# Rest-row scores in four wide matmuls in place of sixteen narrow ones, and no spare products at the turn of the first memory half

## The chip, the cores and the metric

The kernel runs on one NeuronCore of one Trainium2 chip. The metric is device time in microseconds, lower is better; the time before is 2300.26 us, the median of three runs (2291.55 to 2302.47). Every operand in HBM and the output are bf16; sums are in fp32.

## The reference

The output mixes two branches, row by row, with a gate g = sigmoid of x times a vector. Branch B is a feed-forward layer: (gelu(x Wg) * (x Wu)) Wd, 1024 to 3584 and back, over 2048 rows. Branch A is the one that the change touches. It is a recurrence over 64 segments of 32 rows with a memory of 8 rows, 32 heads of 128:

```python
mem = mem0
for s in range(n_seg):                       # 64 segments
    xs = x[:, s*32:(s+1)*32, :]
    h = concatenate([mem, xs], axis=1)       # 8 + 32 = 40 rows
    q, k, v = h @ Wq, h @ Wk, h @ Wv         # 32 heads of 128
    scores = (q . k) * 128**-0.5             # 40 x 40 for each head
    scores = where(mask, scores, -1e9)       # causal; the memory rows see all
    o = (softmax(scores) @ v) @ Wo
    mem = o[:, :8, :]                        # feeds the next segment
    outs.append(o[:, 8:, :])
return g * concatenate(outs) + (1 - g) * B
```

A segment needs the memory rows of the one before, so the segments run one after the other, and for each one all of Wq, Wk, Wv and Wo (8 MB each) passes through the core, as far as it isn't resident.

## The kernel before

The program is written as a list of operations in an order laid out by hand; a small tracker adds semaphore waits from the regions that each operation reads and writes, and each engine then runs its own operations in that order.

**Rows.** Of a segment's 40 rows, 32 go through the recurrent projections: 24 rows of x (`NR`) and the 8 memory rows, in `hT`. The other 8 rows of x, the "rest" (`NB`), need no memory for q, k and v; they are projected for four segments at a time by `fill` (lines 835 to 845; the matmuls stand on L841) from `hR`, leave through `fill_evac` and `fill_put`, lie in HBM scratch (`qk_scr`, `v_scr`) and come back for a segment as `qkr` and `vB`. In `qkr` and `kT` the last columns belong to these rest rows.

**Halves and order.** The 32 heads are two halves of 16. A head in a half has two indices, j and g (0 to 3 each): g is the group of 32 PE columns and 32 PSUM partitions in which it is computed, j its place along the free axis. A segment walks through the stages k, q, (second part of o of the segment before), v for the first half, then k, q, o, v, o for the other. `walk` lists these steps, `proj` (L771 for k, q and v, L787 and L804 for o) issues the matmuls of a step, and `plan(s)` hangs everything else on a step with `on(...)`. Weights stream in 512 KB pieces on the SP queue as their slots come free; 8 matmuls deep, four column groups run side by side with 32 rows of h as the stationary operand.

**Scores.** `scores(u)` works on one half: 16 heads in the PSUM bank `SS`, 128 partitions by four blocks (one for each j) of 80 columns. In block j, columns 0 to 39 are the 32 recurrent rows of head (j, g) against its 40 keys, on partitions 32g to 32g+31; columns 40 to 79 are its 8 rest rows, on partitions 32g to 32g+7. `mask` (L687) first writes the mask `mS` into all four blocks by a matmul with the identity, then 16 matmuls of 32 rows and 16 of 8 rows, 40 columns each, add the products (L700). The softmax is two reductions, an add, an exponential and two products over 128x320 (L706 to L714). DVE then transposes the probabilities in blocks of 32x32, in two instructions of 128x256 (L720): `pAB` has the columns of the recurrent keys in its first half and those of the rest keys in its second, and in `tAB` the queries of head (j, g) must stand at columns 64j to 64j+39 of each half, where `attend` takes them as the moving operand (L729 with `vA`, L737 with `vB`). `attend` for a segment's first half of heads is hung on the first step of o, the scores on the last step of v ahead of it; between them PE runs 68 matmuls of the projections. For the second half they are hung on ("o", 0, 4) and ("o", 1, 0).

**The turn.** When o of a segment is done, `fold(s, b)` adds the two partial sums of one memory half on DVE (L815, L816) and `next_mem(s, b)` transposes it on PE (L825) and copies it into the next `hT` (L828), which the next segment's k needs. At the turn of the first memory half, ahead of step ("k", 0, 0) of the next segment, `plan` puts more work between these: where a segment has two fills, the eight fill matmul groups of the second in two portions of four; in the other 33 of the 63 turns the spare products, `warm(5)` and `warm(2)` (L847 to L855, matmuls on L851): 20 and 8 matmuls of 128x32 by 128x512 whose result in bank `B0` nobody reads.

After the recurrence the rest rows go through Wo (L1027), and then branch B runs in four blocks of 512 rows (L1077, L1131, L1112), with the gate's mix at its ends.

Of the kernel before, what the change touches and what calls it, by code (L numbers as in the profile page):

```python
# [8 lines left out]
ALU = mybir.AluOpType  # L9
# [201 lines left out]
def bass_gated_mix__memory_aug_recurrent_mem_tr__geglu_ffn__prompt_kernel(  # L211
# [21 lines left out]
    NB = SEG - NR  # L233
# [7 lines left out]
    NEG = -1.0e9  # L241
    LQ = 40
# [3 lines left out]
    with ExitStack() as es:  # L246
# [20 lines left out]
        PB = [es.enter_context(nc.psum_tensor(f"pb{i}", [128, 512], FP32)) for i in range(8)]  # L267
# [197 lines left out]
        for g in range(4):  # L465
            q = slice(32 * g, 32 * g + 32)


            pw(mS, lambda e, q=q: sel(e, mS[q, 0:NR], ALU.is_ge, NEG, 0, [[-1, NR]], 1))
            pw(mS, lambda e, q=q: sel(e, mS[q, 32:40], ALU.is_ge, NEG, -NR, [[0, NB]], 1))  # L470

            pw(mS, lambda e, q=q: sel(e, mS[q, 72:80], ALU.is_ge, NEG, 0, [[-1, NB]], 1))
        op("act", lambda e: e.preload_act_table_set("natural_log_exp_and_others"))


# [10 lines left out]
        assert cur[0] <= top  # L486
        memT = al("memT", [128, 64], at=oRc.off)

        def tr_mem(e):
            for kc in range(KC):  # L490
                ins = e.transpose(PBV[5][:, kc * 8:(kc + 1) * 8], pm[0:8, kc * 128:(kc + 1) * 128], ident[0:8, 0:8])
            return ins
# [58 lines left out]
        for n in range(8):  # L551
            first(at_step(0, "k", 0, n))
            if n + 3 < NPX:
                load_x(n + 3)
        op("pe", tr_mem, rd=[pm.r(), ident.r()], wr=[BK(5)])
        op("dve", lambda e: e.tensor_copy(memT[:, :], PBV[5][:, 0:64]), rd=[BK(5)], wr=[memT.r()])
        do_x(0)
        load_h(0, "pool")
# [132 lines left out]
        def scores(u, masked=True):  # L691
            if not masked:
                mask()

            def f(e):
                for n, c in ((32, 0), (8, 40)):
                    for j in range(4):
                        for g in range(4):
                            x = 8 * (4 * j + g)
                            ins = e.matmul(PB[SS][32 * g:32 * g + n, j * 80 + c:j * 80 + c + LQ],  # L700
                                           lhsT=qT[:, j, g, :] if n == 32 else qkr[:, 2 * u, x:x + 8],
                                           rhs=kT[:, j, g, :], start=False, stop=True, skip_group_check=True)
                return ins
            op("pe", f, rd=[qT.r(), qkr.r(256 * u, 256 * u + 128), kT.r()], wr=[BK(SS)])
            op("pool", lambda e: e.memset(pAB[:, 256:544].bitcast(FP32), 0.0), wr=[pAB.r(256)])
            op("dve", lambda e: e.tensor_reduce(nm, sS, AX.X, ALU.max, negate=True), rd=[BK(SS)], wr=[st8.r(0, 8)])  # L706
            op("dve", lambda e: e.tensor_tensor(out=sS, in0=sS, in1=b8(nm, LQ), op=ALU.add), rd=[BK(SS), st8.r(0, 8)], wr=[BK(SS)])  # L707
            op("act", lambda e: e.activation(E8[:, :, :].rearrange("p a c -> p (a c)"), PB[SS][:, 0:320], ACTF.Exp, scale=scale),  # L708
               rd=[BK(SS)], wr=[E8.r()])
            op("dve", lambda e: e.tensor_reduce(sm, E8[:, :, :], AX.X, ALU.add), rd=[E8.r()], wr=[st8.r(8, 16)])  # L710
            op("dve", lambda e: e.reciprocal(sm, sm), rd=[st8.r(8, 16)], wr=[st8.r(8, 16)])
            op("dve", lambda e: e.tensor_tensor(out=pAB[:, 0:256].rearrange("p (a c) -> p a c", a=8), in0=E8[:, :, 0:32], in1=b8(sm, 32), op=ALU.mult),
               rd=[E8.r(), st8.r(8, 16)], wr=[pAB.r(0, 256)])
            fin = op("dve", lambda e: e.tensor_tensor(  # L714
                out=pAB[:, 256:544].rearrange("p (j a) -> p j a", j=4)[:, :, 0:64].rearrange("p j (c k) -> p j c k", c=2)[:, :, :, 0:8],
                in0=E8[:, :, 32:40].rearrange("p (j c) k -> p j c k", c=2),
                in1=sm.rearrange("p (j c) -> p j c", c=2).unsqueeze(3).to_broadcast([128, 4, 2, 8]), op=ALU.mult),
               rd=[E8.r(), st8.r(8, 16)], wr=[pAB.r(256)])
            for c in (0, 256):
                op("dve", lambda e, c=c: e.transpose(tAB[:, c:c + 256], pAB[:, c:c + 256]), rd=[pAB.r(c, c + 256)], wr=[tAB.r(c, c + 256)], after=[fin])  # L720

        def attend(u, by=((2, "act"), (3, "dve"), (0, "act"), (1, "dve")), b3=SS):
            bo = (B0, B1, B2, b3)
# [120 lines left out]
                out.append(lambda f=f, w=w: op("pe", f, rd=[h.r(), w.r()], wr=[BK(b)]))  # L844
            return out

        def warm(n):  # L847
            def f(e):
                for x in range(4 * n):
                    g = x % 4  # L850
                    ins = e.matmul(PB[B0][32 * g:32 * g + 32, :], lhsT=hR[:, 7, :], rhs=spare[:, g * 512:(g + 1) * 512],  # L851
                                   start=True, stop=True)
                return ins
            spare = slots[home["q", 0, 7]]
            op("pe", f, rd=[hR.r(224), spare.r()], wr=[BK(B0)])  # L855

        def fill_evac(m, u, G, b, st):
            st = stage[st]
            if m == "v":
                act_copy(st[:, :], PB[b][:, :], [BK(b)], [st.r()])  # L860
                for g in range(4):
                    op("pool", lambda e, g=g: e.dma_start(
                        v_scr[4 * G:4 * G + 4, :, 4 * g:4 * g + 4, u, :].rearrange("s i j c -> (s i) j c"),
                        st[32 * g:32 * g + 32, :].rearrange("p (j c) -> p j c", j=4)), rd=[st.r()], wr=[("D", "v", G, g, u)], lane=f"fv{g}")
            else:
                act_copy(st[:, :], PB[b][:, :], [BK(b)], [st.r()])

        def fill_put(m, u, G, st, bank=TT):
            if m == "v":
                return  # L870
            st = stage[st]
            turn(st, bank)
            op("dve", lambda e: e.tensor_copy(st[:, :].rearrange("p (i x c) -> p x i c", i=4, x=16),
                                              PBV[bank][:, 0:512].rearrange("p (x i c) -> p x i c", x=16, i=4)), rd=[BK(bank)], wr=[st.r()])
            m4 = 3 * u if m == "q" else 1 + u
            op("pool", lambda e: e.dma_start(qk_scr[:, 4 * G:4 * G + 4, m4, :], st[:, :].rearrange("p (i y) -> p i y", i=4)),
               rd=[st.r()], wr=[("D", "qk", G, m, u)], lane="fq")
# [14 lines left out]
        def some(fs, n):  # L892
            return lambda: run(fs, n)
# [6 lines left out]
        def plan(s):  # L900
# [8 lines left out]
            def on(m, r, n, *fs, s=s):  # L909
                at.setdefault((s, m, r, n), []).extend(fs)  # L910
# [80 lines left out]
                return  # L991
            nx = dict(s=s + 1)
            on("k", 0, 0, lambda: fold(s, 0), **nx)
            on("k", 0, 0, some(f2, 4) if two else lambda: warm(5), **nx)
            on("k", 0, 0, lambda: next_mem(s, 0), **nx)
            on("k", 0, 0, some(f2, 4) if two else lambda: warm(2), **nx)
            if two:
                on("k", 0, 0, lambda: fill_evac(*fl[1], B0, ua), **nx)
            on("q", 0, 2, lambda: fold(s, 1), **nx)
            if two:  # L1000
# [175 lines left out]
```

## Time and profile before

| what | value |
|---|---|
| median of three runs | 2300.26 us |
| the profiled execution, as timed | 2308.1 us |
| its span, first to last instruction | 2306.3 us |
| mean granted PE clock | 0.983 |
| HBM read and written | 596.85 MB and 36.63 MB |
| 200 to 1650 us: PE busy, DMA share, rate | 1345.9 of 1450 us, 0.93, 334 GB/s |
| L700, rest rows: 2048 matmuls | 37.4 us busy |
| L700, recurrent rows: 2048 matmuls | 37.1 us busy |
| L851, spare products: 924 matmuls | 64.6 us busy |
| L720, DVE transposes: 256 | 98.7 us busy, 424 ns each |

A busy time is the time in which at least one instruction of the group ran; matmuls overlap, four column groups at a time, so 4096 matmuls of some 180 ns each make far less than their sum. "Idle before" in a group's row is the engine's own idle time ahead of it, with what released it; a name with "issue" means that nothing in the profile held the engine up.

The span has three parts: the start, to some 120 us; the recurrence, to some 1650 us, about 24 us for a segment; and branch B with the rest rows' projection, where PE runs long matmuls back to back.

### The profile page before, as it was taken

What the parts mean: (1) busy time and instruction counts of PE and PEld (TensorE: products, weight loads), DVE (VectorE), ACT (ScalarE), POOL (GpSimd) and SP (SyncE); (2) the same over time, 40 slices, a digit from 0 to 9 for tenths busy, and PEclk for the clock granted to TensorE, in tenths of its full rate; (3) what the DMA queues carried; (4) which work ended last, traced back from release to release, by engine and by line L of the source; (5) the groups of instructions that cost most, each with busy time, mean ns of one, the idle gap of its engine ahead of it and who ended that gap; (6) DMA issues with size and microseconds to landing.
All of it is one profiled execution on the core that took longest, in us unless ns stands there. A gap on an engine that the chain in (4) does not pass through costs nothing.

```text
span 2306.3 us, 74586 instructions
## 1 busy us (share of the span) xinstructions
PE 2119.9 (92%) x33852; PEld 1048.7 (45%) x33852; DVE 1028.8 (45%) x2440; ACT 541.4 (23%) x1111; POOL 423.7 (18%) x821
## 2 busy tenths in 40 slices
PE   4598999999999999999999999998899999999999
PEld 2244444444444444444444444444464444444444
DVE  3343444454444444544444444454316446163462
ACT  1122222222222222222222222221113123032130
POOL 4422212222222222222222222221100000000000
PEclk8799999999999999999999999999899999999999
DMA  9989999898998999999989899999964440903520
GB/s 375 354 298 327 334 341 358 321 354 320 327 330 325 340 336 316 344 325 355 332 325 354 312 331 341 317 340 324 342 204 143 150 151 10 291 20 125 172 87 19
DMA packets 237579, 638.34 MB, mean 277 GB/s; under 512 B 22440, under 2 KB 91304, under 8 KB 230480
## 3 DMA queue, kind: packets, MB, share of 16 engines
q1 hardware_dynamic: 213440, 596.58, 72.4%
q0 software_dynamic: 13888, 26.31, 3.5%
q10 hardware_dynamic: 9936, 10.69, 1.4%
q8 instruction: 266, 4.36, 0.8%
q14 instruction: 49, 0.40, 0.0%
HBM read 596.85 MB, written 36.63 MB: 275 GB/s over the span
## 4 chain that ended last, share of the span: by engine, by line
PE 70%; DMA 19%; issue 4%; DVE 4%; ACT 2%; POOL 1%; ACTq 0%; SPq 0%; POOLq 0%
PE pb L771 23%; PE pb L1077 15%; DMA sl<-in_A_Wv_dram 7%; PE pb L1131 5%; PE pb L841 5%; PE pb L804 4%; PE pb L787 4%; PE pb L673 3%; DMA qkr<-qk_scr 3%; PE pb L1027 3%; PE pb L1112 2%; PE pb L851 2%; DMA wall<-wg_scr 2%; DMA xr_scr<-xr 1%; DMA o_scr<-oRc 1%
## 5 line engine op out<-in xcount | busy, mean ns | idle before, releaser
L771 PE MATMUL pb<-sl,hT 128*32 128x512 bf16 x12288 | 778.4, 383 | 28.8 <-issue 16.9
L771 PEld LDWEIGHTS pb<-sl,hT 128*32 128x32 bf16 x12288 | 337.5, 97 | 331.6 <-issue 50.8
L841 PE MATMUL pb<-sl,hR 128*32 128x512 bf16 x3072 | 225.3, 392 | 4.1 <-issue 3.2
L1077 PE MATMUL pb<-xT,wg 128*128 128x512 bf16 x896 | 211.7, 379 | 0.7
L1077 PE MATMUL pb<-xT,wu 128*128 128x512 bf16 x896 | 211.7, 379 | 0.0
L804 PE MATMUL pb<-wall,oT 128*32 128x256 bf16 x4056 | 150.9, 275 | 22.9 <-issue 8.5
L787 PE MATMUL pb<-wall,oT 128*32 128x512 bf16 x2048 | 152.4, 387 | 17.1 <-issue 9.5
L656 ACT ACTIVATE kS<-pb 128x512 bf16<-128x512 f32 x127 | 75.8, 597 | 384.3 <-PE pb L771 364.9
L815 DVE COPY part<-pb 64x256 f32<-64x256 f32 x128 | 54.0, 422 | 247.9 <-PE pb L804 246.9
L754 POOL COPY oRc<-oT 128x128 bf16<-128x128 bf16 x128 | 96.4, 753 | 359.2 <-DVE oT L659 357.0
L1131 PE MATMUL pb<-wd,GT 128*128 128x512 bf16 x672 | 146.0, 379 | 1.7 <-DMA wd<-in_B_w_down_dram 1.7
L1085 ACT ACTIVATE s<-pb 128x512 f32<-128x512 f32 x112 | 66.8, 596 | 311.9 <-PE pb L1077 311.9
L708 ACT ACTIVATE E<-pb 128x320 bf16<-128x320 f32 x128 | 55.9, 437 | 352.9 <-DVE pb L707 352.9
L1077 PEld LDWEIGHTS pb<-xT,wg 128*128 128x128 bf16 x896 | 87.2, 98 | 108.0 <-DVE GT L1093 3.7
L1077 PEld LDWEIGHTS pb<-xT,wu 128*128 128x128 bf16 x896 | 87.7, 98 | 105.7
L804 PEld LDWEIGHTS pb<-wall,oT 128*32 128x32 bf16 x4056 | 100.6, 96 | 74.9 <-ACT oT L656 25.9
L1086 DVE SCALAR_TENSOR_TENSOR tp<-s,pb 128x512 f32<-128x512 f32 x112 | 77.0, 687 | 124.2 <-ACT s L1085 124.0
L659 DVE CAST oT<-pb 128x160 bf16<-128x160 f32 x256 | 76.5, 320 | 111.7 <-PE pb L737 111.7
L659 DVE COPY kT<-pb 128x512 bf16<-128x512 bf16 x128 | 54.4, 425 | 159.8 <-PE pb L673 159.5
L880 POOL COPY kT<-qkr 128x128 bf16<-128x128 bf16 x128 | 37.3, 291 | 466.3 <-DVE kT L659 222.6
L841 PEld LDWEIGHTS pb<-sl,hR 128*32 128x32 bf16 x3072 | 82.3, 98 | 70.7 <-issue 20.8
L1090 DVE SCALAR_TENSOR_TENSOR tp<-tp,pb 128x512 f32<-128x512 f32 x112 | 77.1, 688 | 78.6 <-ACT tp L1089 78.6
(100 smaller groups left out, 2286.8 us busy)
## 6 DMA issues: line engine op xcount, KB each, us to landing
sl<-in_A_Wv_dram SPq DMA_DIRECT2D x128, 1024.0 KB, 10.8
wall<-wg_scr SPq DMA_DIRECT2D x53, 1536.0 KB, 9.2
sl<-in_A_Wk_dram SPq DMA_DIRECT2D x64, 1024.0 KB, 5.9
sl<-in_A_Wq_dram SPq DMA_DIRECT2D x64, 1024.0 KB, 9.0
wall<-wo_scr SPq DMA_DIRECT2D x120, 512.0 KB, 6.0
wd<-in_B_w_down_dram SPq DMA_DIRECT2D x42, 1024.0 KB, 5.4
sl<-in_A_Wv_dram SPq DMA_DIRECT2D x75, 512.0 KB, 11.1
wall<-in_A_Wo_dram SPq DMA_DIRECT2D x41, 512.0 KB, 7.9
```

The costliest lines, as they stand in the source:

```text
L656: op("act", lambda e: e.activation(o, i, ACTF.Copy), rd=rd, wr=wr)
L659: op("dve", lambda e: e.tensor_copy(o, i), rd=rd, wr=wr, after=after)
L673: ins = e.transpose(PBV[bank][:, j * 128:(j + 1) * 128], st[:, j * 128:(j + 1) * 128], ident[:, :])
L754: op("pool", lambda e: e.tensor_copy(oRc[:, :, 16 * u:16 * u + 16].rearrange("p c x -> p x c"), oT[:, :, :, 32:40].rearrange("p g j c -> p ...
L771: ins = e.matmul(PB[bk][32 * g:32 * g + 32, :], lhsT=h[:, i, :], rhs=w[:, g * 512:(g + 1) * 512], start=(n == 0), stop=(n == 7))
L787: ins = e.matmul(PB[XO][32 * g:32 * g + 32, :], lhsT=oT[:, j, x, 0:32], rhs=wall[:, na:nb + 1:nb - na, c:c + 256], start=(n == 0 and hp == 0),
L804: ins = e.matmul(PB[XO][32 * g:32 * g + 32, 256 * b:256 * b + 256], lhsT=oT[:, j, x, 0:32], rhs=w[:, c:c + 256], start=False, stop=(n % 4 ...
L841: ins = e.matmul(PB[b][32 * g:32 * g + 32, :], lhsT=h[:, k[2], :], rhs=w[:, g * 512:(g + 1) * 512], start=(n == 0), stop=(n == 7))
L1077: ins = e.matmul(PB[bk][:, 0:FB], lhsT=w[:, kc, cc:cc + 128], rhs=xT[:, :, :, kc, :].rearrange("p t i c -> p (t i) c"), start=(kc == 0), s ...
L1086: op("dve", lambda e, hg=hg, t=t: e.scalar_tensor_tensor(out=t[:, :], in0=s1[:, :], scalar=1.0, in1=hg, op0=ALU.add, op1=ALU.mult), rd=[BK ...
L1090: op("dve", lambda e, hu=hu, t=t: e.scalar_tensor_tensor(out=t[:, :], in0=t[:, :], scalar=1.0, in1=hu, op0=ALU.add, op1=ALU.mult), rd=[BK( ...
L1131: ins = e.matmul(PB[bank[2 * k + hf]][:, :], lhsT=GT[:, j, tb * 128:(tb + 1) * 128], rhs=w[:, jj, hf * 512:(hf + 1) * 512], start=(j == 0) ...
```

## The change

Three things.

1. The rest rows of a half are no longer scored head by head. For each column group g one matmul has all 32 rest rows of its four heads (8 rows each, j = 0 to 3) as the stationary operand and the 160 keys of the four heads as the moving one, and writes columns 40 to 79 of all four blocks. Of its 32 rows in block j only rows 8j to 8j+7 are head j's own; the others are products across heads that nobody uses. Sixteen matmuls with their weight loads become four. So that the rows stand like that, `fill_put` copies q in the order (segment, g, j, row) in place of (segment, j, g, row); k keeps its order.
2. With the rest rows at partitions 32g+8j in block j, the mask has to hold for all 16 groups of 8 partitions (`mT`, made once on POOL, transposed on PE with `tr_mem` and copied to `mS`; four POOL selections go), and the transposes have to shift them: `halves` transposes the rest part of each half first, with a target stride of 56 columns, so that the rows of head j land at 64j+32, and then the recurrent part at 64j, over what was written too much. Two DVE instructions of 128x256 become four of 128x128. The second of a pair waits for the first.
3. `warm` is gone: in the 33 turns without a second fill nothing stands between `fold`, `next_mem` and the next k.

```diff
@@ -469,7 +469,6 @@
             pw(mS, lambda e, q=q: sel(e, mS[q, 0:NR], ALU.is_ge, NEG, 0, [[-1, NR]], 1))
             pw(mS, lambda e, q=q: sel(e, mS[q, 32:40], ALU.is_ge, NEG, -NR, [[0, NB]], 1))
 
-            pw(mS, lambda e, q=q: sel(e, mS[q, 72:80], ALU.is_ge, NEG, 0, [[-1, NB]], 1))
         op("act", lambda e: e.preload_act_table_set("natural_log_exp_and_others"))
 
 
@@ -486,7 +485,12 @@
         assert cur[0] <= top
         memT = al("memT", [128, 64], at=oRc.off)
 
+        mT = al("mT", [128, 16, NB])
+        pw(mT, lambda e: e.memset(mT[0:NB, :, :], 0.0), True)
+        pw(mT, lambda e: sel(e, mT[0:NB, :, :], ALU.is_ge, NEG, 0, [[0, 16], [1, NB]], -1))
+
         def tr_mem(e):
+            e.transpose(PBV[5][:, 64:64 + NB], mT[0:NB, :, :].rearrange("p x i -> p (x i)"), ident[0:NB, 0:NB])
             for kc in range(KC):
                 ins = e.transpose(PBV[5][:, kc * 8:(kc + 1) * 8], pm[0:8, kc * 128:(kc + 1) * 128], ident[0:8, 0:8])
             return ins
@@ -552,7 +556,8 @@
             first(at_step(0, "k", 0, n))
             if n + 3 < NPX:
                 load_x(n + 3)
-        op("pe", tr_mem, rd=[pm.r(), ident.r()], wr=[BK(5)])
+        op("pe", tr_mem, rd=[pm.r(), mT.r(), ident.r()], wr=[BK(5)])
+        op("dve", lambda e: e.tensor_copy(mS[:, 72:80], PBV[5][:, 64:64 + NB]), rd=[BK(5)], wr=[mS.r(72, 80)])
         op("dve", lambda e: e.tensor_copy(memT[:, :], PBV[5][:, 0:64]), rd=[BK(5)], wr=[memT.r()])
         do_x(0)
         load_h(0, "pool")
@@ -693,13 +698,14 @@
                 mask()
 
             def f(e):
-                for n, c in ((32, 0), (8, 40)):
-                    for j in range(4):
-                        for g in range(4):
-                            x = 8 * (4 * j + g)
-                            ins = e.matmul(PB[SS][32 * g:32 * g + n, j * 80 + c:j * 80 + c + LQ],
-                                           lhsT=qT[:, j, g, :] if n == 32 else qkr[:, 2 * u, x:x + 8],
-                                           rhs=kT[:, j, g, :], start=False, stop=True, skip_group_check=True)
+                for j in range(4):
+                    for g in range(4):
+                        ins = e.matmul(PB[SS][32 * g:32 * g + 32, j * 80:j * 80 + LQ], lhsT=qT[:, j, g, :],
+                                       rhs=kT[:, j, g, :], start=False, stop=True, skip_group_check=True)
+                for g in range(4):
+                    ins = e.matmul(PB[SS][32 * g:32 * g + 32, 0:320].rearrange("p (j c) -> p j c", j=4)[:, :, LQ:80],
+                                   lhsT=qkr[:, 2 * u, 32 * g:32 * g + 32],
+                                   rhs=kT[:, :, g, :], start=False, stop=True, skip_group_check=True)
                 return ins
             op("pe", f, rd=[qT.r(), qkr.r(256 * u, 256 * u + 128), kT.r()], wr=[BK(SS)])
             op("pool", lambda e: e.memset(pAB[:, 256:544].bitcast(FP32), 0.0), wr=[pAB.r(256)])
@@ -716,8 +722,11 @@
                 in0=E8[:, :, 32:40].rearrange("p (j c) k -> p j c k", c=2),
                 in1=sm.rearrange("p (j c) -> p j c", c=2).unsqueeze(3).to_broadcast([128, 4, 2, 8]), op=ALU.mult),
                rd=[E8.r(), st8.r(8, 16)], wr=[pAB.r(256)])
-            for c in (0, 256):
-                op("dve", lambda e, c=c: e.transpose(tAB[:, c:c + 256], pAB[:, c:c + 256]), rd=[pAB.r(c, c + 256)], wr=[tAB.r(c, c + 256)], after=[fin])
+            def halves(k, w, after):
+                return [op("dve", lambda e, c=c: e.transpose(tAB[:, c + 32 * k:c + 32 * k + 4 * w].rearrange("p (j x) -> p j x", j=4)[:, :, 0:32],
+                                                             pAB[:, c:c + 256].rearrange("p (j k x) -> p j k x", j=4, k=2)[:, :, k, :]),
+                           rd=[pAB.r(c, c + 256)], wr=[tAB.r(c, c + 256)], after=[x]) for c, x in zip((0, 256), after)]
+            halves(0, 64, halves(1, 56, [fin, fin]))
 
         def attend(u, by=((2, "act"), (3, "dve"), (0, "act"), (1, "dve")), b3=SS):
             bo = (B0, B1, B2, b3)
@@ -844,16 +853,6 @@
                 out.append(lambda f=f, w=w: op("pe", f, rd=[h.r(), w.r()], wr=[BK(b)]))
             return out
 
-        def warm(n):
-            def f(e):
-                for x in range(4 * n):
-                    g = x % 4
-                    ins = e.matmul(PB[B0][32 * g:32 * g + 32, :], lhsT=hR[:, 7, :], rhs=spare[:, g * 512:(g + 1) * 512],
-                                   start=True, stop=True)
-                return ins
-            spare = slots[home["q", 0, 7]]
-            op("pe", f, rd=[hR.r(224), spare.r()], wr=[BK(B0)])
-
         def fill_evac(m, u, G, b, st):
             st = stage[st]
             if m == "v":
@@ -870,8 +869,8 @@
                 return
             st = stage[st]
             turn(st, bank)
-            op("dve", lambda e: e.tensor_copy(st[:, :].rearrange("p (i x c) -> p x i c", i=4, x=16),
-                                              PBV[bank][:, 0:512].rearrange("p (x i c) -> p x i c", x=16, i=4)), rd=[BK(bank)], wr=[st.r()])
+            to = st[:, :].rearrange("p (i g j c) -> p j g i c", i=4, g=4, j=4) if m == "q" else st[:, :].rearrange("p (i j g c) -> p j g i c", i=4, j=4, g=4)
+            op("dve", lambda e: e.tensor_copy(to, PBV[bank][:, 0:512].rearrange("p (j g i c) -> p j g i c", j=4, g=4, i=4)), rd=[BK(bank)], wr=[st.r()])
             m4 = 3 * u if m == "q" else 1 + u
             op("pool", lambda e: e.dma_start(qk_scr[:, 4 * G:4 * G + 4, m4, :], st[:, :].rearrange("p (i y) -> p i y", i=4)),
                rd=[st.r()], wr=[("D", "qk", G, m, u)], lane="fq")
@@ -991,10 +990,11 @@
                 return
             nx = dict(s=s + 1)
             on("k", 0, 0, lambda: fold(s, 0), **nx)
-            on("k", 0, 0, some(f2, 4) if two else lambda: warm(5), **nx)
+            if two:
+                on("k", 0, 0, some(f2, 4), **nx)
             on("k", 0, 0, lambda: next_mem(s, 0), **nx)
-            on("k", 0, 0, some(f2, 4) if two else lambda: warm(2), **nx)
             if two:
+                on("k", 0, 0, some(f2, 4), **nx)
                 on("k", 0, 0, lambda: fill_evac(*fl[1], B0, ua), **nx)
             on("q", 0, 2, lambda: fold(s, 1), **nx)
             if two:
```

## The prediction

> **What bounds the kernel now.** I read the page first, then PE's waits, then the timeline of single stretches. The page:
>
> ```profile
> PE 2119.9 (92%) x33852; PEld 1048.7 (45%) x33852; DVE 1028.8 (45%) x2440; ACT 541.4 (23%) x1111; POOL 423.7 (18%) x821
> ...
> DMA  9989999898998999999989899999964440903520
> ...
> q8 instruction: 266, 4.36, 0.8%
> ```
>
> PE is busy for 92% of the span of 2306.3 us, and in the recurrence (to about 1650 us) the DMA engines are nearly full beside it. The line that matters most is the smallest: 266 instruction packets. 4.36 MB over 266 is 16 KB each; 33852 matmuls and 33852 weight loads are 67704 instructions, and 67704 over 266 is about 255. PE's program comes in blocks of some 256 instructions, one packet for each. What that costs is in PE's waits, among rows for other causes:
>
> ```profile
> PE pb L771 <- issue: 16.9, 20, 1.9
> ...
> PE pb L787 <- issue: 9.5, 8, 2.4
> PE pb L804 <- issue: 9.0, 12, 1.7
> PE pb L700 <- issue: 8.7, 10, 2.2
> ```
>
> "Issue" means that nothing in the profile held PE up. With L841 (3.2, 5 times), L673 (3.1, 4) and L737 (2.9, 3) these are 53.3 us in 62 waits, more than any engine or DMA costs PE. That they are block boundaries shows on the timeline of PE:
>
> ```profile
> 762.24 1.91 PE L771 MATMUL pb<-sl,hT 128*32 128x512 bf16 x31 [1.69 <-issue]
> ...
> 768.57 0.61 PE L851 MATMUL pb<-sl,hR 128*32 128x512 bf16 x6 [0.34 <-issue]
> ```
>
> Between these two waits PE runs 127 matmuls with their loads, one block to within a few. They strike whatever line stands there, so their price depends on how long a block lasts, not on what PE computes. Do they reach the end? From the end of one turn to the next (starts of L816) a segment without such a wait takes 22.72 us (791.32 to 814.04); the one with the wait of 2.40 takes 26.78 (837.26 to 864.04), of which 1.66 is the half clock seen below. So they pass through almost whole; over segments 11 to 60 I find 0.94 us of period for 1 us of wait.
>
> **Fewer instructions (both edits).** The spare products go in 33 turns: 28 matmuls and 28 loads each, 1848. In each of 128 score steps 16 pairs for the rest rows become 4: 24 instructions less, 3072. Together 4920 of 67704, 19 packets. Nearly all lie in the recurrence, where 226 packets cover 1460 us (190 to 1650), 6.46 us a block, 6.2 without the waits. About 18 blocks fewer there stretch a block to some 6.75, by 0.5. If a packet takes as long to come as now, each of the 62 waits is shorter by 0.5, 31 us at most; about 18 of them are shorter than that and give only their length, which leaves 28. A packet queues behind the weight loads, and the loads get denser as PE gets faster, so I take **-24**. Bounds: 0 (packets later by as much) and -45 (all but the longest waits).
> The Trainium skill, Runtime: NRT & Kernel Launch, "Instruction fetch mechanics", gives the same 16 KB blocks of 256 instructions and says that crossing one is mostly hidden; the rows above disagree, with 53.3 us unhidden. By the page this term would be 0.
>
> **The turn of the first half.** PE waits for fold and next_mem; the spare products fill the wait:
>
> ```profile
> 790.52 1.25 PE L851 MATMUL pb<-sl,hR 128*32 128x512 bf16 x20
> 791.32 0.42 DVE L816 TENSOR_TENSOR a_bf<-pb,part 64x256 bf16<-64x256 f32 x1
> 791.79 0.23 PE L825 MATMUL pb<-ident,a_bf 64*128 64x64 bf16 x2
> 791.95 0.61 PE L851 MATMUL pb<-sl,hR 128*32 128x512 bf16 x8
> 792.06 0.18 DVE L828 COPY hT<-pb 128x32 bf16<-128x32 bf16 x1 [0.32 <-PE pb L825]
> 792.39 0.60 PE L771 MATMUL pb<-sl,hT 128*32 128x512 bf16 x8
> ```
>
> The first twenty cost nothing: L825 starts 0.05 after L816 ends, at best 0.03 is to be had. The eight behind it cost 0.10: L771 starts 0.15 after L828 ends, a wait alone takes 0.05. 33 turns x 0.10, and 0.03 in about 20 of them: **-4** (bounds -7, where a half clock lengthened the products themselves at 181 and 1608 us, and 0).
> What they hid is PE's clock. A stretch of 3.4 us with little matmul work is followed by one at half clock:
>
> ```profile
> 540.24:543.65 3.41, 1.46 (x31) 0.57 (x23) 2.31 (x7) 0.44 (x1) 0.09 (x1) 1.00 1.05 398
> 854.28:857.68 3.40, 1.00 (x21) 0.60 (x23) 2.27 (x7) 0.44 (x1) 0.05 (x1) 1.00 1.04 395
> 857.69:861.09 3.40, 3.40 (x40) 1.58 (x32) 0.00 (x0) 0.04 (x1) 0.00 (x0) 0.50 1.02 426
> ```
>
> Columns: length, busy PE, PEld, DVE, ACT, POOL, clock, DMA share, GB/s. PE idle for 2.40 of 3.40 halves the next stretch; 1.95 idle did not. There are three such half stretches from 190 to 1650 us (687, 858, 1605), each behind an issue wait. A turn without the products idles 1.35 (790.69 to 791.76, 792.02 to 792.30), so it needs 0.6 to 1 more in the same stretch. Laying the shorter waits at random over the segments I expect five half stretches in place of three: 2 x 1.5 us, **+3**. Bounds: -4 (none left) and +48 (each of the 33 turns, 1.45 each).
> The Trainium skill, TensorE: Matmul & The Clock Gate, "Why this matters for your kernels", allows idle gaps up to about 3 us between bursts; by that a turn costs nothing. The trace is stricter, since gaps in one stretch add up.
>
> **Scores.** PE issues 32 matmuls of 40 columns from 799.77 and L771 follows at 799.99: 0.22, of which the 16 of the rest rows have 0.11. Four of 160 columns, one for each column group side by side, take as long as 160 columns do: L771's sets of four stream 512 in 0.216, so 0.07. PE gains 0.04 where it is late.
>
> **The transposes.** Two of 128x256 become four of 128x128, and attend waits for the last. The view of one score step:
>
> ```profile
> 803.15 0.77 DVE L720 STREAM_TRANSPOSE tAB<-pAB 128x256 bf16<-128x256 bf16 x2
> 803.79 0.27 PE L729 MATMUL pb<-tAB,vA 32*128 32x40 bf16 x16
> 803.98 0.21 PE L737 MATMUL pb<-tAB,vB 32*128 32x64 bf16 x4
> ```
>
> L737 starts 0.06 after the transposes end (803.92): in the first attend of a segment DVE, not PE, sets this point. DVE's pieces fit 0.155 + elements/0.96 ns (219 ns for 64, 425 for 256), and one follows the other after about 0.06 + elements/0.96. Four of 128 end after 3 x 0.19 + 0.29 = 0.87, in place of 0.77: +0.10 in 63 first attends, **+6**. The waits of the second pair on the first end while another piece runs. The short score step saves nothing there. In the second attend ACT's vA comes last (L729 <- ACT vA, 37.3 us of PEld's waits), so the longer transposes hide behind it; without that cover they would cost as much again. PE keeps its 0.04 in 64 of those: **-2**. No row shows a strided transpose. Bounds: 0 if the pieces cost as their elements, +0.65 a step (+41) if each takes 424 like one of 256; I take the fit, since L714 and L712 on the same data follow it.
> Nothing else counts: fill_put's copy (L873, 425 ns, 61 times) keeps its 512 elements in runs of 8 with one dimension more; hidden by POOL's and DVE's slack except in turns like 813.1 us. Even 0.27 more in 31 of them is 8, in the range. The mask work replaces four POOL pieces of 0.19 by two ahead of the first loads' arrival.
>
> **Sum**: -24 - 4 + 3 + 6 - 2 = -21 on the profiled execution (span 2306.3, 2308.1 with what lies around it). The median shown is 2300.26, 8 below that execution; I put the difference on the median: **2279**.
>
> **Rivals.**
> - *The waits stay.* Packets come later by what a block gains, or DMA, 93% busy from 200 to 1650 us, fills the time with load waits. For it: the DMA row, and 24 us of PEld waits for Wv. Against it: consecutive segments at 22.7 to 23.2 us, so the loads can keep up. Only +3 +6 -6 remains: 2303. The Trainium skill's rule on fetching (Runtime: NRT & Kernel Launch) ends here too. Chance 0.20.
> - *The clock gate decides* (slower). Place: the 33 turns. If a turn alone is enough for the gate, 33 x 1.45 = 48: -24 - 4 + 48 + 6 - 2 = +24, 2324. It turns slower from 20 half stretches on (17 more). Against it: 1.95 idle went unpunished. Chance 0.06.
> - *Strided transposes are dear* (slower). At 424 each: +41 in the first attends, and the second's cover (L729 starts 0.5 behind the first transpose in the tightest) fails too, some +10: -24 - 4 + 3 + 51 - 2 = +24, 2324. From 0.43 a step it decides. Chance 0.09.
> - *The waits all but vanish*: -45 in place of -24, and the clock drops behind them with it, -4: 2251. For it: the waits are the tail of a queue, and a tail shrinks faster than its mean. Chance 0.12.
>
> **Chances and range.** Forecast 0.53, between 2262 and 2294 by the give and take of its terms. Range 2254 to 2306: it takes in the vanishing waits' edge and the first rival, and leaves out the slower two and some of the fast end. A measurement here tells about 0.5% (11.5 us). Faster by more: the forecast's 0.48 and 0.12, 0.60. Within: 0.05 and 0.18, 0.23. Slower: 0.06, 0.09 and 0.02, 0.17.
>
> **What would show it.** 247 instruction packets in place of 266; PE's issue waits near 25 to 30 us; L720 256 more times with about 0.29 us each, and L737 in the first attend still close behind them; L771 0.05 behind L828 in the turn; about five half stretches in the recurrence. If the packets fall to 247 and the issue waits stay above 45 us, the main step is wrong.

## The result, and the profile after

| | before | after |
|---|---|---|
| median (20 runs each, taken in turn) | 2300.86 us | 2307.44 us |
| ratio after/before, 95% interval | | 1.0029 [1.0016, 1.0042] |
| profiled execution as timed, span | 2308.1, 2306.3 us | 2311.71, 2309.9 us |
| mean granted PE clock | 0.983 | 0.980 |

By the bound of 0.5% there is no change; the interval lies wholly above 1, so what there is is a loss, of 4 to 10 us. The forecast was 2279, 28 us too low. Of the page of the changed kernel: the instruction count, the engines, the clock and the instruction packets:

```profile
span 2309.9 us, 69920 instructions
...
PE 2069.2 (90%) x31393; PEld 982.4 (43%) x31393; DVE 1044.2 (45%) x2697; ACT 541.9 (23%) x1111; POOL 423.4 (18%) x819
...
PEclk9699999999999999999999999998999999999999
...
q8 instruction: 247, 4.05, 0.7%
```

PE has 4918 instructions and 51 us of busy time less, and the packets fell to 247. The work went away; the time didn't. What PE waits for now (line, what released it: us in all, times, longest):

```profile
PE pb L834 <- DVE a_bf L825: 36.3, 44, 1.1
...
PE pb L780 <- DMA sl<-in_A_Wv_dram: 17.3, 23, 2.0
PE pb L703 <- POOL kT L879: 15.8, 18, 3.2
PE pb L813 <- DMA wall<-wg_scr: 10.5, 16, 1.4
PE pb L738 <- DVE tAB L726: 9.3, 7, 3.7
...
PE pb L780 <- issue: 4.2, 7, 1.4
PE pb L850 <- issue: 2.9, 6, 0.9
```

(L780 was L771, L834 was L825, L837 was L828, L703 and L706 were L700, L726 was L720, L738 was L729, L813 was L804, L850 was L841.) The issue waits, the costliest cause before, are now 13.5 us in 22. At the top stand the turn, without its spares, and three rows of loads; L703's wait for kT is one too, since kT's copy on POOL waits in turn for the transfer of qkr. All of PE's idle gaps above 0.06 us from 190 to 1650 us, summed by releaser over the trace (the half clock counts a stretch whole if it begins in there):

```
                     before    after
all                    98.1    147.7
issue                  54.4     14.1
weight transfers       15.0     46.3
kT (transfer of qkr)    7.4     14.7
a_bf and hT (turn)      4.1     45.3
transposes (tAB)        1.2      9.6
half clock, us         10.2     34.1
```

So the issue waits did go (-40.3), and waits for loads rose by about as much (+38.6). The spares' time turned into waits of the turn. PE's busy time between 200 and 1650 us fell by 48.5 (1345.9 to 1297.4), its idle time rose by as much. The chain of waits from 200 to 1600 us, of before and then of after, puts the shift in shares of the path:

```profile
by line: PE pb L771 35.4%; DMA sl<-in_A_Wv_dram 11.6%; PE pb L841 6.7%; PE pb L804 6.7%; PE pb L787 5.9%; issue 5.1%; PE pb L673 4.6%; DMA qkr<-qk_scr 3.8%; PE pb L851 2.9%; DMA wall<-wg_scr 2.7%; DMA o_scr<-oRc 2.0%; PE pb L700 1.6%; PE pb
```

```profile
by line: PE pb L780 27.2%; DMA sl<-in_A_Wv_dram 16.0%; DMA wall<-wg_scr 11.5%; PE pb L813 4.5%; DMA qkr<-qk_scr 4.4%; PE pb L796 4.2%; DMA o_scr<-oRc 4.1%; PE pb L678 3.9%; PE pb L850 3.5%; issue 3.2%; DMA sl<-in_A_Wq_dram 2.3%; ACT vA L661
```

Wv and wg together went from 14.3% to 27.5%. Where in a segment that happens is seen in windows laid from the end of the fold, of before (first three lines) and of after (columns as in the prediction: length, busy PE, PEld, DVE, ACT, POOL, clock, DMA share, GB/s):

```profile
719.60:721.60 2.00, 1.77 (x38) 0.81 (x34) 0.59 (x2) 0.00 (x0) 0.59 (x1) 1.00 0.58 164
721.60:724.20 2.60, 2.60 (x68) 1.62 (x64) 0.65 (x2) 0.60 (x1) 0.00 (x0) 1.00 0.35 88
724.20:730.00 5.80, 5.76 (x123) 2.64 (x119) 2.18 (x7) 1.19 (x2) 2.36 (x5) 1.00 0.99 348
```

```profile
716.10:718.10 2.00, 1.59 (x28) 0.68 (x32) 0.56 (x2) 0.00 (x0) 0.54 (x1) 1.00 0.72 241
718.10:720.70 2.60, 2.60 (x68) 1.62 (x61) 0.22 (x1) 0.60 (x1) 0.00 (x0) 1.00 0.35 69
720.70:726.50 5.80, 5.75 (x108) 2.53 (x111) 2.26 (x7) 1.19 (x2) 2.31 (x5) 1.00 0.98 344
```

The transfers have one gap in a segment, in the some 4 us behind the turn, while PE uses up the weights whose slots SP is to load next. After it they run nearly full until the next turn: with segments 12 to 58 cut into 24 parts each, the mean share of the first four is 0.74, 0.48, 0.28 and 0.71 before (0.77, 0.57, 0.40 and 0.89 after) and 0.91 to 1.03 in all others. Of before's issue waits there (43.0 us), 29.5 lie in the full stretch from 4.6 to 20 us behind the fold, 5.7 ahead of it, 7.8 behind it.

The turn itself, on the timeline of after:

```profile
788.33 0.42 DVE L825 TENSOR_TENSOR a_bf<-pb,part 64x256 bf16<-64x256 f32 x1
788.80 0.23 PE L834 MATMUL pb<-ident,a_bf 64*128 64x64 bf16 x2 [1.09 <-DVE a_bf L825]
789.07 0.17 DVE L837 COPY hT<-pb 128x32 bf16<-128x32 bf16 x1 [0.32 <-PE pb L834]
789.30 1.48 PE L780 MATMUL pb<-sl,hT 128*32 128x512 bf16 x24 [0.27 <-DVE hT L837]
```

PE waits 1.09 and 0.27 there, and L780 starts 0.06 behind the end of L837.

### The profile page after: what moved, and what is told of

The parts are those of the page before. It is cut to its first block, busy times and chain, and to the rows that moved or that the text cites. A ratio compares the mean times of both kernels' runs of the same rounds, so it can differ in the third digit from the quotient of the medians.

```text
span 2309.9 us, 69920 instructions
## 1 busy us (share of the span) xinstructions
PE 2069.2 (90%) x31393; PEld 982.4 (43%) x31393; DVE 1044.2 (45%) x2697; ACT 541.9 (23%) x1111; POOL 423.4 (18%) x819
## 4 chain that ended last, share of the span: by engine, by line
PE 56%; DMA 32%; DVE 5%; issue 3%; ACT 2%; POOL 1%; SPq 0%; ACTq 0%; POOLq 0%; DVEq 0%
PE pb L780 18%; PE pb L1077 15%; DMA sl<-in_A_Wv_dram 10%; DMA wall<-wg_scr 7%; PE pb L1131 5%; DMA qkr<-qk_scr 3%; PE pb L813 3%; DMA o_scr<-oRc 3%; PE pb L796 3%; PE pb L678 3%; PE pb L850 3%; PE pb L1027 2%; PE pb L1112 2%; DMA sl<-in_A_Wq_dram 1%; DMA xr_scr<-xr 1%
## 5 line engine op out<-in xcount | busy, mean ns | idle before, releaser
L780 PE MATMUL pb<-sl,hT 128*32 128x512 bf16 x12288 | 776.1, 385 | 36.6 <-DMA sl<-in_A_Wv_dram 17.3
L780 PEld LDWEIGHTS pb<-sl,hT 128*32 128x32 bf16 x12288 | 312.5, 97 | 361.4 <-DMA sl<-in_A_Wv_dram 39.8
L850 PE MATMUL pb<-sl,hR 128*32 128x512 bf16 x3072 | 220.7, 392 | 3.5 <-issue 2.9
L813 PE MATMUL pb<-wall,oT 128*32 128x256 bf16 x4056 | 154.1, 278 | 33.7 <-DMA wall<-wg_scr 10.5
L813 PEld LDWEIGHTS pb<-wall,oT 128*32 128x32 bf16 x4056 | 96.9, 97 | 95.8 <-ACT oT L661 25.8
L664 DVE COPY kT<-pb 128x512 bf16<-128x512 bf16 x128 | 54.4, 425 | 160.9 <-PE pb L678 160.9
L726 DVE STREAM_TRANSPOSE tAB<-pAB 128x128 bf16<-128x128 bf16 x512 | 114.0, 280 | 4.4
```

The source lines that it names most:

```text
L664: op("dve", lambda e: e.tensor_copy(o, i), rd=rd, wr=wr, after=after)
L726: return [op("dve", lambda e, c=c: e.transpose(tAB[:, c + 32 * k:c + 32 * k + 4 * w].rearrange("p (j x) -> p j x", j=4)[:, :, 0:32], pAB[: ...
L780: ins = e.matmul(PB[bk][32 * g:32 * g + 32, :], lhsT=h[:, i, :], rhs=w[:, g * 512:(g + 1) * 512], start=(n == 0), stop=(n == 7))
L813: ins = e.matmul(PB[XO][32 * g:32 * g + 32, 256 * b:256 * b + 256], lhsT=oT[:, j, x, 0:32], rhs=w[:, c:c + 256], start=False, stop=(n % 4 ...
L850: ins = e.matmul(PB[b][32 * g:32 * g + 32, :], lhsT=h[:, k[2], :], rhs=w[:, g * 512:(g + 1) * 512], start=(n == 0), stop=(n == 7))
```

## The experiments

Two theories after the result. **Loads**: a segment's 8 MB are the bound from the gap to the next turn, and PE's time counts only where it decides when the gap ends. **Turn**: the missing products cost the clock and something more, and without that the change would gain. Each run is said to be "before" or "after" with an edit. Ratios stand against runs of the kernel before on the same chip, whose median there was 2298.98 to 2304.48 us; between chips the ratios are compared, not the times.

**The parts of the change alone.** e1 is before without the spares; e2 is after with `warm` back; e3 is after with 7 products of full width (128x128 by 128x512) for the 28.

```diff
-            on("k", 0, 0, some(f2, 4) if two else lambda: warm(5), **nx)
+            on("k", 0, 0, some(f2, 4) if two else lambda: None, **nx)
             on("k", 0, 0, lambda: next_mem(s, 0), **nx)
-            on("k", 0, 0, some(f2, 4) if two else lambda: warm(2), **nx)
+            on("k", 0, 0, some(f2, 4) if two else lambda: None, **nx)
```

> The kernel before without the spare products alone; scores as before. Clock theory (the fetch gain is real, and the empty turns spend it at half clock): half clock from 190 to 1650 us rises from 10 to 30 us or more, that is +10 us of PE time against some -6 us of instruction waits and -4 us in the turns: 2300 to 2306, with instruction waits still above 40 us. Load theory (the weight loads set the recurrence, so that PE time moves little either way): 2297 to 2303, PE's waits for weights up from 15 us by as much as the instruction waits fall.

> The changed kernel with the spare products put back: the four wide score matmuls, the mask and the four transposes remain. Clock theory: half clock back to some 10 us, instruction waits near 25 us, and the time falls by about 15 us, to 2282 to 2290. Load theory: instruction waits fall the same, but PE's waits for weights and for qkr grow by most of it; the time stays within 0.3% of before, 2294 to 2305.

> The changed kernel with other spare products: five and two matmuls of 128 weight columns by 512 (the identity as weights) in place of 20 and 8 of 32 columns; the same time on PE in 14 instructions for 56. Clock theory: the best of all, 2278 to 2288, no more half clock than before and about 235 to 250 instruction packets. Load theory: as the scores alone, 2292 to 2304.

| | us | ratio | packets | issue | weights + kT | half clock |
|---|---|---|---|---|---|---|
| e1 | 2318.68 | 1.0073 [1.0047, 1.0100] | 259 | 45.3 | 38.9 | 20.5 |
| e2 | 2316.63 | 1.0076 [1.0047, 1.0104] | 254 | 15.6 | 62.8 | 6.8 |
| e3 | 2318.8 | 1.0070 [1.0045, 1.0094] | 249 | 6.3 | 69.5 | 13.7 |

(The last three columns are in us and taken as in the table of PE's gaps.) All three lie above every range given for them, of either theory. Each half alone is slower than both together. In e2 the turn is as before and the half clock no more than before, and it still loses: the clock isn't what ate the gain. Issue fell by 38.8, load waits rose by 40.4, and PE's two largest rows in e2 are loads:

```profile
PE pb L780 <- DMA sl<-in_A_Wv_dram: 26.7, 37, 2.1
PE pb L703 <- POOL kT L889: 26.6, 29, 2.1
```

e3 takes the issue waits nearly away and is no faster. Of the issue waits, leaving out the spares took 9.1 us (e1, 1848 instructions), the new scores 38.8 (e2, 3072). In e1 the spares' place is a wait:

```profile
PE pb L825 <- DVE a_bf L816: 37.4, 48, 1.1
```

**The transposes alone**, without their shift: before with four adjacent pieces of 128 columns.

```diff
-            for c in (0, 256):
-                op("dve", lambda e, c=c: e.transpose(tAB[:, c:c + 256], pAB[:, c:c + 256]), ...
+            for c in (0, 128, 256, 384):
+                op("dve", lambda e, c=c: e.transpose(tAB[:, c:c + 128], pAB[:, c:c + 128]), ...
```

> The kernel before with the two DVE transposes of 128x256 cut into four of 128x128 of adjacent columns; nothing else. Prices the transposes alone. If they cost what their fit says, 0.10 us in each of 63 first attends: +6 us, 2303 to 2309, if PE's time passes through; within 3 us of before if the loads set the time (PE then only waits elsewhere). The pieces should take about 290 ns.

2303.22 us, 1.0008 [0.9984, 1.0031]: no loss that can be told, but the interval takes in the +6 us too.

**Less to load.** The Wv piece of slot ("v", 0, 4) is fetched once and not for each segment, which takes 0.5 MB off a segment's 8.0 (one half is then multiplied with the other half's piece): e5 is before with it, e6 after, e7 e2.

```diff
         def due(n):
+            if n == home["v", 0, 4]:
+                return None, False
```

> The kernel before, but the Wv piece of 512 KB with index 4 is loaded once and then kept for both halves (so one half is multiplied with the other half's rows): 0.5 MB less of some 7.8 MB in each segment, PE's work the same. Load theory: the time falls, but not by the whole 1.4 us a segment that 0.5 MB takes, since instruction waits remain: 2230 to 2270. Clock theory (PE is the bound and loads are not): little, 2285 to 2300.

> The changed kernel with the same Wv piece loaded once. Load theory: falls by more than the kernel before does, since its instruction waits are few: 10 to 25 us below the light kernel before. Clock theory: as far above the light kernel before as the changed kernel is above before, +2 to +10 us, and the half clock stays.

> The changed kernel with the spare products put back and the same Wv piece loaded once. Load theory: the predicted fetch gain is seen here in full: 20 to 30 us below the light kernel before. Clock theory: 10 to 20 us below the light changed kernel, by the half clock alone.

e5 2283.45 (0.9894 [0.9867, 0.9922]), e6 2275.46 (0.9866 [0.9844, 0.9888]), e7 2292.26 (0.9943 [0.9924, 0.9963]). Against their full forms e5 gives 1.1%, e6 1.6%, e7 1.3%. So loads are on the path in all three, and most in after: with 6% off them it stands 8 us ahead of before with the same, where in full it stands 7 behind; the intervals of e5 and e6 overlap, so the order itself isn't settled. But they are not the only bound. By the ratios 24, 38 and 30 us came back of some 90 that the transfers took (64 x 1.4, an estimate), so the load theory's ranges were missed: e5 stands above its range, e6 is 8 us below e5 and not 10 to 25, and e7 is 9 above e5 and not 20 to 30 below. Even with lighter loads the new scores alone don't win.

**Less for PE to do.** After, with only two of a fill's eight matmul groups.

```diff
+                if thin and 0 < n < 7:
+                    out.append(lambda: None)
+                    continue
```

> The changed kernel with six of the eight matmul groups left out of each fill in the recurrence (84 fills, so 504 sets of four, 109 us of PE's stream, and 4032 instructions): loads, copies and transfers stay. Load theory: PE's work is not the bound, and the time falls by less than 30 us. If PE is the bound: it falls by 80 us or more.

2315.36, 1.0051 [1.0031, 1.0071]. Some 109 us of PE's stream are gone and nothing is gained. It isn't a clean test: the fills had also covered the softmax chain (PE's waits for ACT rose to 48.4 us, for tAB to 21.7) and the clock (99 us at half).

**More for PE to do**, at two places: three products of 128x128 by 128x512, 0.65 us in a segment, 41 us in all. e9 puts them in the full stretch, e10 right behind the turn.

```diff
+            if s > 0:
+                on("k", 1, 4, lambda: extra(3))
```

```diff
             on("k", 0, 0, lambda: fill_evac(*fl[1], B0, ua), **nx)
+            on("k", 0, 0, lambda: extra(3), **nx)
```

> The changed kernel with three more matmuls of 128x128 by 128x512 (0.65 us of PE's stream) in 63 segments, in the middle of the second k stage, where the DMA engines are full. Load theory (the loads of a segment run back to back from the turn on, and PE's time inside that stretch is free): within 10 us of the changed kernel, 2303 to 2317. If PE's time counts everywhere: 63 x 0.65 = +41 us, 2348.

> The same three matmuls in the same kernel, but at the turn, between next_mem of the first half and the first k step, where the DMA engines have run dry and wait for PE to free the first slots. Load theory: the whole 0.65 us counts in 63 turns, +35 to +45 us, 2340 to 2352. If PE's time counts everywhere: the same, so that only the pair tells.

e9 2319.87 (1.0064 [1.0040, 1.0088]), e10 2429.77 (1.0529 [1.0501, 1.0558]). Over after's 1.0029 that is 8 us, as the load theory had it, and 115 us, far above the 35 to 45 of both theories. Most of e10 is no product: in 30 turns with a second fill they wait for the bank that ACT empties,

```profile
PE pb L859 <- ACT 1S L661: 35.6, 15, 3.7
PE pb L859 <- ACT 0S L661: 31.5, 15, 3.3
```

which is 67 us, and the half clock is 61 us there. The traces, split by the kind of turn (28 of each kind, from the third turn on), show how a delay of the first k step passes on:

```
              with a second fill            without
         k behind hT   segment     k behind hT   segment
after       0.59        24.23         0.05        24.33
e9          0.59        24.38         0.05        24.40
e10         3.72        27.59         0.47        24.67
```

(us; from the end of hT's copy to the first matmul of k, median, and the mean segment from that turn to the next, with a standard error near 0.2.) With a second fill k starts 3.13 us later and the segment is 3.36 longer: such a delay passes whole, but its cause is the bank. Without one, k starts 0.42 later and the segment is 0.34 longer, where e9's products make it 0.07 longer; the errors leave open whether so short a delay costs more behind the turn than in the full stretch.

**Place in memory.** e11 is e2, e12 is before, with 1.44 MB of unused scratch ahead of the tables, in case the changed kernel's buffers lie worse.

```diff
+        pad_scr = nc.dram_tensor("pad_scr", [8, 90112], BF16)
```

> The changed kernel with the spare products put back (2317 us where it was measured), with an unused scratch of 1.44 MB declared ahead of the others, so that they lie elsewhere in HBM; one small transfer to it after the recurrence. If its slower weight packets come from where the data lie: the time moves by more than 8 us, towards 2300. If they come from the order and times of the transfers: 2311 to 2322.

> The kernel before with the same unused scratch. If places in HBM matter: more than 8 us off before. If not: 2294 to 2307.

e11 1.0060 [1.0038, 1.0082] and e12 0.9992 [0.9974, 1.0010]: no effect.

**Versions that free the turn.** If time behind the turn counts most, the second fill's last four groups and its evacuation should go later (v1 on before, v3 on after), the first fill's copy and its transfer too, with the eight products left out (v2), and the eight products behind next_mem should go alone (v4). v5 is v1 with v4; v6 is v5 with the new scores.

```diff
             if two:
-                on("k", 0, 0, some(f2, 4), **nx)
-                on("k", 0, 0, lambda: fill_evac(*fl[1], B0, ua), **nx)
+                on("k", 0, 2, some(f2, 4), **nx)
+                on("k", 0, 2, lambda: fill_evac(*fl[1], B0, ua), **nx)
```

```diff
             on("k", 0, 0, lambda: next_mem(s, 0), **nx)
-            on("k", 0, 0, some(f2, 4) if two else lambda: warm(2), **nx)
+            on("k", 0, 0, some(f2, 4) if two else lambda: None, **nx)
```

> The kernel before with the second four matmul groups of the second fill, and its evacuation, moved from the turn to behind the first two k steps (30 turns). At the turn k starts some 0.55 us earlier in each, and the first loads with it. Load theory: -10 to -20 us, 2284 to 2294. If PE's time counts alike everywhere: nothing is removed, within 4 us of before.

> v1, and the eight spare products behind next_mem left out, and the copy of fill_put behind next_mem's copy on DVE (its transposes into another bank). Load theory: 0.10 us more in 33 turns and about 0.1 in 30: 4 to 8 us below v1, 2278 to 2290, if the emptier turn does not bring more half clock (then 2288 to 2300).

> The changed kernel with v1's move of the second fill. Load theory: as much as v1 gains, -10 to -20 us against the changed kernel: 2288 to 2298. If the changed kernel's slower weight packets stay, it ends 5 to 15 us above v1.

> The kernel before without the eight spare products behind next_mem; the twenty ahead of it stay, so that a turn idles some 0.3 us and not 1.35. Load theory with the clock as the price of the empty turn: 33 x 0.10 us at the turn, 2294 to 2300, and half clock stays near 10 us. If leaving products out costs by itself, as it did with all of them: 2305 to 2318.

> The kernel before with only the twenty spare products ahead of next_mem, and the second half of the second fill moved behind the first k steps: the edits of v4 and v1 together. If turn time adds up: -10 and -4, 2286 to 2292. If v1's edit loses at half clock what it wins (20 us of half clock against 10): as v4, 2291 to 2297.

> v5's turn with the changed kernel's scores, mask and transposes. If instruction waits saved under full loads are given back and the transposes cost little: within 6 us of v5. If the scores by themselves bring the slower loads seen in the kernel with the spare products put back: 8 to 20 us above v5. If they bring what was forecast: 15 us or more below.

| | us | ratio | issue | weights + kT | half clock |
|---|---|---|---|---|---|
| v1 | 2298.44 | 0.9982 [0.9960, 1.0003] | 43.2 | 23.4 | 20.5 |
| v2 | 2366.39 | 1.0264 [1.0224, 1.0304] | 34.4 | 17.8 | 71.7 |
| v3 | 2297.32 | 0.9974 [0.9956, 0.9992] | 11.6 | 53.1 | 34.1 |
| v4 | 2292.85 | 0.9961 [0.9940, 0.9981] | 49.6 | 26.2 | 10.2 |
| v5 | 2294.85 | 0.9968 [0.9951, 0.9985] | 44.3 | 26.7 | 13.7 |
| v6 | 2305.89 | 1.0017 [1.0004, 1.0031] | 16.7 | 54.7 | 13.7 |

v4 has the lowest median, under both kernels and a little below the 2294 to 2300 expected, by taking out 8 of the 28 products and nothing else; the intervals of v3 and v5 overlap its own. The turn theory is borne out in part. The late fill lets k start 0.54 us earlier in 30 turns (0.05 for 0.59 behind hT's copy), 16 us in all: v1 gained 4 of them, short of the 10 to 20 expected and with an interval that reaches 1; v3 gained 13 on after (0.9974 for 1.0029, intervals apart). The edits don't add: v5 is no better than v4. v2 lost 61 us, for a reason of its own, a buffer: ACT's next evacuation into the stage waited for the later transfer out of it (ACT's waits):

```profile
ACT kS L656 <- DMA qk_scr<-kS: 189.6, 26, 10.4
```

v5 to v6 is the price of the new scores with one and the same turn: 1.0017 over 0.9968, +11 us, in the range of 8 to 20 that was given for slower loads.

## Why the prediction was wrong

**The step that failed is the first term, fewer instructions (-24).** Its working on the packets held: 247 of them, as forecast, and the issue waits fell by 40 us, more than the 28 worked out. What failed is "so they pass through almost whole", the 0.94 us of period for 1 us of wait. That was a slope between segments of one kernel. It isn't the slope for all segments at once: of 50 segments before (11 to 60) 12 had no issue wait and took 23.15 us in the mean; after, 31 had none and took 23.98. With PE early everywhere the weights come last. (That a lone segment without the wait lives on a lead that others gave the loads would explain it; no run shows that.) After, e2 and e3 show it the same way: 39 to 48 us less issue, 39 to 47 us more load waits (weights and kT). Consecutive segments at 22.7 to 23.2 us were taken as proof that "the loads can keep up"; after's mean over segments 12 to 58 is 24.07 us, before's 24.08 (the 3.6 us between the two profiled spans lie outside, 3.3 of them in the last five segments). One profile of each doesn't place so small a loss: e12, which does in the recurrence what before does, has 23.99. The outcome is the rival "The waits stay" in its second form, load waits in place of issue waits, which had 0.20 and gave 2303, 4 below the result. The Trainium skill (Runtime: NRT & Kernel Launch, "Instruction fetch mechanics") called a block crossing mostly hidden; its term of 0 comes nearer the sum, but not by its reason, since before shows 54 us of such waits.

Part of the loss is in the loads' own pace. Means of a segment (12 to 58), mean idle time of the 16 DMA engines in it and rate while they are busy (the bytes are the same 8.0 MB, so two of the columns give the third):

```
         period us   DMA idle us   GB/s
before     24.08        1.94      362.1
after      24.07        1.62      356.3
e2         24.11        1.50      354.1
v4         23.91        1.63      359.3
v3         23.81        1.29      355.3
```

The changed kernels fill the gap better, and then move bytes 1.6 to 2.2% slower; a 4 KB weight packet takes 181.8 ns before, 184.8 after, 187.7 in e2 (means, 200 to 1600 us). A gap shorter by 0.3 to 0.4 us and some 22 us of transfers that are 0.3 to 0.5 us longer cancel. Why the packets get longer isn't settled. It is no chance of one profile (e12 has 181.7 ns), not the place in memory (e11, e12), and not the new scores as such: e1 and v5, with the old ones, move 356.0 and 356.4 GB/s.

**The turn (-4).** That the eight products behind next_mem delay the turn by 0.10 was right: k starts 0.16 us behind hT's copy before, 0.05 in v4 and after. v4 measured -9 (interval -14 to -4), where 3.3 was put on them; the rest is open. In the profiles the segments behind the edited turns are 0.06 us shorter (24.32 to 24.26), those behind the others, from which nothing was taken, 0.21 (24.14 to 23.93). That the first twenty "cost nothing" held, but taking them out does: e1 against v4, 1.0073 to 0.9961, is +26 us. Of that the half clock accounts for 3 stretches more (20.5 to 10.2 us; 3 x 1.45 = 4.4) and load waits for 12.7 (38.9 to 26.2). The rest is open, and so is why the same removal doesn't cost under the new scores, where after stands at 1.0029 and e2 at 1.0076.

**The half clock (+3)** was mis-sized: 34.1 us, ten stretches, where five were forecast and three were before; 7 x 1.45 = 10. Two of them:

```profile
875.62:879.00 3.38, 3.38 (x49) 1.36 (x53) 1.25 (x4) 0.53 (x3) 1.27 (x3) 0.50 0.92 344
1466.12:1469.50 3.38, 2.98 (x32) 1.17 (x34) 0.00 (x0) 0.00 (x0) 0.00 (x0) 0.50 0.55 153
```

What mis-sized it is the bound: the prediction took it that between 1.95 and 2.40 us of idle are needed, so that a turn's 1.35 wants 0.6 to 1 more. The other two of before's half stretches (687 and 1605 us) already stood behind 1.93 and 1.76 idle:

```profile
683.60:687.00 3.40, 1.47 (x17) 0.57 (x21) 0.52 (x2) 0.66 (x3) 0.29 (x1) 1.00 0.60 233
1601.80:1605.20 3.40, 1.64 (x44) 0.72 (x40) 2.02 (x7) 1.09 (x3) 0.93 (x2) 1.00 1.01 394
```

After's ten begin at eight places, behind 1.70 to 2.17 us of idle in 3.4, so that some 0.4 beside a turn can do. The 1.95 that went unpunished shows only that the idle time alone gives no sharp bound. The one at 1466 us stands behind a turn (0.98 and 0.27 idle) with a wait of 0.54 ahead of it in the same stretch. The rival "the clock gate decides" fell all the same: 7 more stretches, not 33, and v3 has as many as after and stands at 0.9974 for after's 1.0029. The Trainium skill (TensorE: Matmul & The Clock Gate, "Why this matters for your kernels") allows gaps of up to about 3 us; in after only one idle gap of PE between 190 and 1650 us is longer (3.2 us, the longest of L703's waits for kT), and half clock begins at eight places.

**Scores and transposes.** Four wide matmuls take 0.07 of PE's stream, as forecast (first line to the next group of L780: 797.01 to 797.08), and the transposes 0.89 for 0.87 forecast:

```profile
797.01 0.24 PE L706 MATMUL pb<-kT,qkr 128*32 128x160 bf16 x4
797.08 4.13 PE L780 MATMUL pb<-sl,hT 128*32 128x512 bf16 x68
...
784.03 0.89 DVE L726 STREAM_TRANSPOSE tAB<-pAB 128x128 bf16<-128x128 bf16 x4
```

The median piece is 269 ns, so "strided transposes are dear" fell. PE's wait for them rose by 8.4 us, near the +6. That four pieces cost nothing that e4 could tell, and that v5 to v6 costs 11 us, points to the loads more than to DVE for the loss of the new scores, but doesn't show it: the load waits rose there by 28.0 us (26.7 to 54.7) for 27.6 less issue, so the 11 us themselves aren't accounted for. The -2 of PE's gain was not measured by itself.

Set side by side, -40 and +39 for the packets, -3 at the turn, +10 for the clock and +8 for the transposes make roughly +14; measured +7 (4 to 10). These are waits and estimates, each by its own price, which leaves out what they hide of one another. So the exchange of issue waits for load waits is shown, three times; why the loads give no more, and what makes up the +7, is open.

## What to carry to other kernels

Before pricing a wait of PE, look whether the DMA engines are full while it stands there; if they are, the time may come back as a load wait, as it did here, whatever a slope between neighbouring segments says. In a loop whose loads run full but for one gap, look for savings first where PE's progress ends that gap, here behind the turn: leaving out eight products there gained 9 us (v4), leaving out 4920 instructions nothing. It is a place to try, not a rule: the 16 us of the late fill gained 13 in one kernel and 4 in the other. Take work that fills a wait out only in parts and measure each, since taking out the twenty ahead of the turn and the eight behind it had opposite signs.

## What the runs showed of the hardware that was not expected

- The issue waits fall much faster than the packets: 54.4 us at 266, 45.3 at 259 (e1), 15.6 at 254 (e2), 14.1 at 247, and 3.4 us in e9, whose 248 packets hold three long products more for each segment.
- At the eight places in after, half clock follows a stretch of 3.4 us with 1.70 to 2.17 us of idle. The idle may lie in pieces: at 1609 us 0.32, 1.43 and 0.43. A stretch with 1.95 went without (before, at 540 us).
- With fewer waits of PE, 4 KB packets on full queues take longer: 181.8 ns before, 187.7 in e2. No run shows why.
- Three products in a segment cost 8 us in the full stretch, and 115 behind the turn, where most of it is waits for a bank.
